# Transposing transfers for two of twelve pairs in a fused linear-attention and MLP kernel

## The chip, the cores and the metric

The kernel runs on one core of a Trainium2 chip. Its engines are TensorE (PE in the profile, its weight loads PEld), VectorE (DVE), ScalarE (ACT), GpSimd (POOL) and SyncE (SP), which here only issues transfers. The metric is device time in microseconds. Every engine works through its own list of instructions in order; they meet through semaphores.

## The reference, cut to what matters

First a recurrent attention with a decaying state, over 4 batches, 8 heads, 768 steps and head size 48, then an MLP with a cosine gate over the 3072 tokens:

```
for t in range(S):
    state = alpha[:, :, t, :, None] * state + einsum('bhd,bhe->bhde', k[:, :, t], v[:, :, t])
    y[:, :, t] = einsum('bhd,bhde->bhe', q[:, :, t], state)

x = y as (3072 tokens, 384)
h = x @ w_in            # 384 -> 2048
g = h * cos(h)
out = g @ w_out         # 2048 -> 384
```

## The kernel before, in words

The work is cut into 12 pairs J = 0 to 11, three to a batch. A pair is 256 steps, two chunks c = 0, 1 of 128; each of the 128 partitions holds two neighbouring steps, its parities e = 0, 1, so partitions 0 to 63 are chunk 0 and 64 to 127 chunk 1. The "ninth pair" is J = 8, the "eleventh" J = 10. For each pair:

- `load` (L105) brings alpha, k, q and v, 384 KB each, on SyncE's queue.
- `ln`, `cums`, `icp` and `exps` (L139 to L208) turn alpha into cumulative products and their inverses. From pair 3 on, the four exponentials of a pair and the logarithm of the next form one session on ScalarE (`eb`), between two loads of function tables.
- `scale_k` (L212) and `scale_q` (L216) multiply k and q by these into bf16 tiles `kh` and `qh`, on POOL or VectorE. There are three buffers of each, 64 columns a head, of which 16 stay zero.
- `trans` (L253 to L261) transposes k and q on TensorE: 4 head pairs x 2 parities x 2 chunks each, 32 transposes into a PSUM tile `T_ps`. `evict_T` (L266) copies each half to the SBUF tile `qkT` (three buffers), on VectorE or ScalarE.
- `scores` (L274) multiplies k by q out of `qkT`, `mask` (L279) evicts them, `outer` (L291) makes the outer products of k and v, `add_state` and `decay_state` (L305 to L313) carry the state.
- `stack_v` (L225) rearranges v by four transfers of 64 KB on SyncE's queue (`vs`).
- `yT` (L340) sums state and score parts, and reads q from `qkT`; `evict_y` (L351) writes the MLP's input.
- `mlp1` (L361), `cosine` (L367), `gate` (L372) and `mlp2` (L390) do the MLP, in four groups of 512 hidden columns. `evict_o` (L402) copies the 384 output columns of each half out of the single PSUM bank "o", into one of four `o_sb` buffers, and `store` (L408) writes 192 KB on SyncE's queue.

PSUM tag "h" is a ring of three two-bank tiles, taken in the order of the calls. `T_ps`, the scores, U, y and the four h tiles of every pair go through it, so a tile waits until the one three places before it has been read.

The order of all work is written out by hand. `PLAN` (L433 on) gives every step of every pair a number; all steps are sorted by it and called in that order, and this is the order of each engine's list, SyncE's among them. The numbers are no times of the chip, only an order. A letter behind a number picks the engine.

Around the two edited places the order of SyncE's list is: load v of pair 11, store of pair 3 half 0, vs of pair 7, store of pair 3 half 1, vs of pairs 8 and 9, store of pair 4 half 1, load k of pair 11, store of pair 5 half 0, vs of pair 10.

Of the kernel before, what the change touches and what calls it, by code (L numbers as in the profile page):

```python
# [10 lines left out]
BF = mybir.dt.bfloat16  # L11
AF = mybir.ActivationFunctionType
ALU = mybir.AluOpType
# [3 lines left out]
def kernel(  # L17
# [10 lines left out]
    nc = tc.nc  # L28
    B, H, S, D = q.shape
    DM, DF = moe_w_in.shape  # L30
    C = 128
    HC = C // 2
# [3 lines left out]
    NP = H // 2  # L36
# [7 lines left out]
    NL, NQ, NV, NS = 4, 3, 3, 2  # L44
    BUF = {"a": 4, "in": 3, "cp": 3, "qkT": 3, "A": 2, "un": 4, "us": 2, "c": 3, "xT": 3, "g": 4}

    consts = ctx.enter_context(tc.tile_pool(name="consts", bufs=1))
    sb = ctx.enter_context(tc.tile_pool(name="sb", bufs=2))
# [15 lines left out]
    for c in range(2):  # L64
        r = slice(HC * c, HC * c + HC)
# [4 lines left out]
    ident_bf = consts.tile([C, C], BF, tag="ident_bf")  # L70
# [8 lines left out]
    lna_t, qh_t, kh_t, vp_t, vs_t = [], [], [], [], []  # L79
    for lst, nm, n in ((lna_t, "lna", NL), (kh_t, "kh", NQ), (qh_t, "qh", NQ), (vp_t, "vp", NV)):  # L80
        for r in range(n):
            t = consts.tile([C, 2, H, 64], BF, tag=f"{nm}{r}", name=f"{nm}{r}")
            nc.vector.memset(t[:, :, :, D:64], 0.0)
            lst.append(t)
    for r in range(NS):
        t = consts.tile([C, 2, H, 64], BF, tag=f"vs{r}", name=f"vs{r}")
        nc.gpsimd.memset(t[:, :, :, D:64], 0.0)
# [9 lines left out]
    a_sb, kqv, cp_sb, icp_sb, qkT_sb, A_sb, c2_sb = {}, {}, {}, {}, {}, {}, {}  # L97
# [73 lines left out]
    def two_banks(name):  # L171
        return ps.tile([C, 2, 512], FP, tag="h", name=name, bufs=3)
# [36 lines left out]

    def scale_k(J, e, eng):  # L210
        icp_ = icp_sb.pop((J, e)).rearrange("p (h d) -> p h d", h=H)
        eng.tensor_tensor(out=kh_t[J % NQ][:, e, :, 0:D], in0=kqv["k", J][:, :, e], in1=icp_, op=ALU.mult)  # L212

    def scale_q(J, e, eng):
        cp = cp_sb[J, e][:, 0:HD].rearrange("p (h d) -> p h d", h=H)
        eng.tensor_tensor(out=qh_t[J % NQ][:, e, :, 0:D], in0=kqv["q", J][:, :, e], in1=cp, op=ALU.mult)  # L216

    def cast_v(J):
        nc.gpsimd.tensor_copy(out=vp_t[J % NV][:, :, :, 0:D].rearrange("s e h d -> s h e d"), in_=kqv.pop(("v", J)))  # L219
# [18 lines left out]
    def evict_vs(J, copy):  # L238
        copy(out=vs_t[J % NS][:, :, :, 0:D],
             in_=vs_ps.pop(J)[:, :, 0:HD].rearrange("s c (h d) -> s c h d", h=H))  # L240
# [12 lines left out]
    def trans(J):  # L253
        T_ps[J] = ps.tile([C, 2, 2 * NP, 2, HC], BF, tag="h", name="T_ps", bufs=3)
        for i, x in ((1, kh_t[J % NQ]), (0, qh_t[J % NQ])):
            for p in range(NP):
                for e in range(2):
                    for c in range(2):
                        r = slice(HC * c, HC * c + HC)
                        nc.tensor.transpose(T_ps[J][:, c, i * NP + p, e, :],  # L260
                                            x[r, e, 2 * p : 2 * p + 2, :].rearrange("s h d -> s (h d)"), ident_bf[r, r])  # L261

    def evict_T(J, c, copy):
        if J not in qkT_sb:
            qkT_sb[J] = sb.tile([C, 2, 2 * NP, C], BF, tag="qkT", name="qkT", bufs=BUF["qkT"])
        copy(out=qkT_sb[J][:, c], in_=T_ps[J][:, c].rearrange("r n e s -> r n (e s)"))  # L266
# [16 lines left out]
    def outer(J):  # L283
        n = 2 if J % NJB < NJB - 1 else 1
        kh, vp = kh_t[J % NQ], vp_t[J % NV]
        U_ps[J] = two_banks("U_ps")
        for p in range(NP):
            for e in range(2):
                for c in range(n):
                    r = slice(HC * c, HC * c + HC)  # L290
                    nc.tensor.matmul(  # L291
                        U_ps[J][:, c, 2 * p * D : 2 * (p + 1) * D].rearrange("r (a d) -> r a d", a=2),
                        kh[r, e, 2 * p : 2 * p + 2, :].rearrange("s h d -> s (h d)"),
                        vp[r, e, 2 * p : 2 * p + 2, 0:D], start=(e == 0), stop=(e == 1))

    U_new = {}
# [50 lines left out]
    def evict_y(J, c, copy):  # L347
        if J not in xT:
            xT[J] = sb.tile([C, KT, T2], BF, tag="xT", name="xT", bufs=BUF["xT"])

        copy(out=xT[J][:, :, c * C : (c + 1) * C].rearrange("r i (t e) -> r i e t", e=2),  # L351
             in_=y_ps[J][:, c, 0 : KT * C].rearrange("r (i e t) -> r i e t", i=KT, e=2))
# [59 lines left out]
    def idle(n):  # L412
# [5 lines left out]
    copies = {"DVE": nc.vector.tensor_copy, "ACT": nc.scalar.copy}  # L418
    mults = {"DVE": nc.vector, "POOL": nc.gpsimd}
    steps = {  # L420
        "load": lambda J, nm: load(nm, J), "w1": load_w1, "w2": load_w2,
        "mula": mul_a, "ln": ln, "cums0": cums0, "cums": cums, "sub": sub, "icp": icp, "exps": exps, "eb": session,
        "sk": lambda J, e, eng="POOL": scale_k(J, e, mults[eng]), "sq": lambda J, e, eng="POOL": scale_q(J, e, mults[eng]),
        "castv": cast_v, "vst": stack_v, "vpe": stack_v_pe,
        "vev": lambda J, eng="DVE": evict_vs(J, copies[eng]), "decay": decay, "trans": trans,
        "evT": lambda J, c, eng="DVE": evict_T(J, c, copies[eng]), "scores": scores, "mask": mask, "outer": outer,
        "add": add_state, "state": decay_state, "yT": yT, "evy": lambda J, c, eng="ACT": evict_y(J, c, copies[eng]),
        "m1": mlp1, "sin": cosine, "gate": gate, "m2": mlp2, "evo": lambda J, c, eng="ACT": evict_o(J, c, copies[eng]),
        "out": store, "idle": idle,
# [68 lines left out]
    }  # L498
    IDLE = [(1501, 16), (7915, 1), (9416, 8), (12569, 4), (14554, 5), (16389, 3), (18254, 3)]

    order = []
    for key, line in PLAN.items():
        kind, *rest = key.split()
        for J, word in enumerate(line.split()):
            if word != "-":
                t, _, eng = word.partition(":")
# [38 lines left out]
```

## Time and profile before

| what | value |
| --- | --- |
| median of 3 runs | 188.16 us (187.92 to 188.28) |
| span of the profiled execution, first to last instruction | 186.5 us |
| median of the runs less that span | 1.66 us |
| TensorE busy | 176.7 us, 95% |
| VectorE busy | 135.4 us, 73% |
| ScalarE busy | 126.5 us, 68% |
| GpSimd busy | 77.1 us, 41% |
| transposes L260 | 384, in groups of 32 |
| evictions L266 | VectorE 16, mean 678 ns; ScalarE 8, mean 1015 ns |
| transfers vs<-vp on SyncE | 36, 64 KB each, 2.1 us to landing |
| stores on SyncE | 23, 192 KB each, 2.6 us to landing |
| granted TensorE clock | 1.000 |

The profiled execution's own time on the device is given by its span only; the median is of other executions of the same program. Groups of instructions are named by line, engine and operation, with what is written before the arrow and what is read behind it. Times in a timeline or a chain count from the start of the span. The chain of waits is found backwards from the last instruction: at each step to what released it, or to the instruction before it on its engine. Transfers issued by SyncE appear as SPq; their duration there is that of the issue and not of the transfer.

### The profile page before, as it was taken

The page shows a single profiled execution, that of the slowest core. Times are in us where ns is not written, and L with a number is a line of the kernel's source. Part 1 is how long each engine was busy: PE and PEld are TensorE (multiplying, and loading weights), DVE is VectorE, ACT ScalarE, POOL GpSimd, SP SyncE. Part 2 cuts the span into 40 slices and gives each one's busy share as a digit, 9 for nine tenths or more (in the row PEclk, how much of TensorE's full clock was granted, in tenths as well). Part 3 has the DMA queues.
Part 4 walks back from the last instruction along what each step waited for, and adds up shares of the span by engine and source line. Part 5 has one row for each costly group of instructions (what it writes and reads, how often), then busy time and mean ns, then how long its engine had stood idle before and what let it go on. Part 6 is the DMA issues. An engine that isn't in the chain of part 4 may idle for free.

```text
span 186.5 us, 5746 instructions
## 1 busy us (share of the span) xinstructions
PE 176.7 (95%) x2467; PEld 126.4 (68%) x2469; DVE 135.4 (73%) x184; ACT 126.5 (68%) x161; POOL 77.1 (41%) x110
## 2 busy tenths in 40 slices
PE   7988799989989999999999999999999999999993
PEld 2434588655667786785688668676867686786872
DVE  7178775589799979698847987794977556754461
ACT  2466876889498986889668999728965264373330
POOL 5079510257645653781896076930360320100000
PEclk9999999999999999999999999999999999999999
DMA  6999999999949979996799932600041005301102
GB/s 152 261 258 165 181 204 237 259 266 265 274 105 304 264 180 245 264 260 167 186 278 278 247 104 46 182 0 4 4 136 47 5 0 158 118 0 66 64 0 84
DMA packets 60137, 29.47 MB, mean 158 GB/s; under 512 B 51024, under 2 KB 60112, under 8 KB 60112
## 3 DMA queue, kind: packets, MB, share of 16 engines
q1 hardware_dynamic: 56256, 25.86, 57.2%
q0 software_dynamic: 3712, 3.15, 11.0%
q8 instruction: 19, 0.31, 0.7%
q10 hardware_dynamic: 144, 0.10, 0.2%
q14 instruction: 6, 0.05, 0.1%
HBM read 25.17 MB, written 4.72 MB: 160 GB/s over the span
## 4 chain that ended last, share of the span: by engine, by line
PE 73%; ACT 15%; DVE 8%; issue 3%; DVEq 0%
PE h_ps L361 31%; PE o_ps L390 24%; PE idle_ps L416 4%; PE y_ps L340 3%; ACT qkT L266 3%; DVE gsb L372 3%; PE T_ps L260 2%; ACT c_sb L367 2%; PE A_ps L274 2%; ACT L136 2%; ACT cp L200 2%; PE U_ps L291 2%; DVE kh L212 2%; ACT icp L192 2%; PE o_last L384 1%
## 5 line engine op out<-in xcount | busy, mean ns | idle before, releaser
L372 DVE TENSOR_TENSOR gsb<-h_ps,c_sb 128x1024 bf16<-128x1024 f32 x48 | 58.1, 1221 | 21.9 <-ACT c_sb L367 21.2
L367 ACT ACTIVATE c_sb<-h_ps,halfpi 128x1024 bf16<-128x1024 f32 x48 | 53.0, 1113 | 26.8 <-PE h_ps L361 23.0
L361 PE MATMUL h_ps<-xT,w 128*128 128x256 bf16 x576 | 66.7, 273 | 1.3 <-ACT xT L351 0.7
L390 PE MATMUL o_ps<-w,gsb 128*128 128x384 bf16 x368 | 66.7, 327 | 0.1
L361 PEld LDWEIGHTS <-w 128*128 128x128 bf16 x576 | 55.6, 98 | 10.1 <-issue 1.6
L390 PEld LDWEIGHTS <-gsb 128*128 128x128 bf16 x368 | 33.8, 98 | 21.2 <-DVE gsb L372 0.6
L313 POOL TENSOR_TENSOR un<-us,c 128x384 bf16<-128x384 f32 x20 | 16.7, 835 | 40.7 <-DVE us L305 29.1
L279 DVE TENSOR_TENSOR A_sb<-A_ps,msk 128x1024 bf16<-128x1024 f32 x24 | 28.9, 1215 | 1.7 <-PE A_ps L274 1.7
L212 POOL TENSOR_TENSOR kh<-k,icp 128x384 bf16<-128x384 f32 x17 | 16.9, 999 | 9.2 <-ACT icp L192 7.8
L216 POOL TENSOR_TENSOR qh<-q,cp 128x384 bf16<-128x384 f32 x15 | 15.0, 1006 | 11.8 <-ACT cp L200 11.8
L149 POOL TENSOR_TENSOR a<-a 128x384 f32<-128x384 f32 x9 | 9.0, 1001 | 12.6 <-DMA a<-in_alpha_dram 12.6
L219 POOL CAST vp<-v 128x768 bf16<-128x768 f32 x12 | 10.1, 841 | 8.8 <-DMA v<-in_v_dram 7.7
L416 PE MATMUL idle_ps<-zeros 128*128 128x512 bf16 x38 | 12.0, 457 | 1.4 <-DVE zeros L52 1.2
L141 ACT ACTIVATE lna<-a 128x768 bf16<-128x768 f32 x12 | 10.2, 847 | 4.6 <-DMA a<-in_alpha_dram 4.6
L266 ACT COPY qkT<-T_ps 128x1024 bf16<-128x1024 bf16 x8 | 8.0, 1015 | 6.9 <-PE T_ps L260 4.4
L136 ACT ACT_TABLE_LOAD x9 | 11.5, 1283 | 0.9 <-PEq L529 0.7
L367 ACT ACT_TABLE_LOAD x9 | 11.5, 1283 | 0.2
L266 DVE COPY qkT<-T_ps 128x1024 bf16<-128x1024 bf16 x16 | 10.8, 678 | 1.1 <-ACT qkT L266 1.1
L305 DVE TENSOR_TENSOR us<-U_ps,un 128x384 f32<-128x384 f32 x16 | 8.7, 550 | 3.8 <-PE U_ps L291 2.8
L402 DVE COPY o_sb<-o_ps 128x384 f32<-128x384 f32 x12 | 6.6, 551 | 6.5 <-PE o_ps L390 6.5
L351 ACT CAST xT<-y_ps 128x384 bf16<-128x384 f32 x12 | 6.7, 594 | 5.6 <-PE y_ps L340 3.8
L351 DVE CAST xT<-y_ps 128x384 bf16<-128x384 f32 x12 | 6.8, 584 | 4.7 <-PE y_ps L340 2.9
(69 smaller groups left out, 159.1 us busy)
## 6 DMA issues: line engine op xcount, KB each, us to landing
k<-in_k_dram SPq DMA_DIRECT2D x12, 384.0 KB, 6.0
a<-in_alpha_dram SPq DMA_DIRECT2D x12, 384.0 KB, 6.1
v<-in_v_dram SPq DMA_DIRECT2D x12, 384.0 KB, 6.0
q<-in_q_dram SPq DMA_DIRECT2D x12, 384.0 KB, 6.3
out_dram<-o_sb SPq DMA_DIRECT2D x23, 192.0 KB, 2.6
vs<-vp SPq DMA_DIRECT2D x36, 64.0 KB, 2.1
w<-in_moe_w_out_dram POOLq DMA_DIRECT2D x4, 384.0 KB, 10.1
w<-in_moe_w_in_dram POOLq DMA_DIRECT2D x4, 384.0 KB, 7.3
```

The source lines that it names most:

```text
L136: nc.scalar.preload_act_table_set("natural_log_exp_and_others")
L212: eng.tensor_tensor(out=kh_t[J % NQ][:, e, :, 0:D], in0=kqv["k", J][:, :, e], in1=icp_, op=ALU.mult)
L216: eng.tensor_tensor(out=qh_t[J % NQ][:, e, :, 0:D], in0=kqv["q", J][:, :, e], in1=cp, op=ALU.mult)
L266: copy(out=qkT_sb[J][:, c], in_=T_ps[J][:, c].rearrange("r n e s -> r n (e s)"))
L279: nc.vector.tensor_tensor(out=A_sb[J][:, c].rearrange("s a p t -> s (a p) t"), in0=A_ps.pop((J, c)).rearrange("s a p t -> s (a p) t"), in1 ...
L313: nc.gpsimd.tensor_tensor(out=u, in0=U_sum.pop(n), in1=c2_sb[J][:, :, c].unsqueeze(3).to_broadcast([C, NP, 2, D]), op=ALU.mult)
L351: copy(out=xT[J][:, :, c * C : (c + 1) * C].rearrange("r i (t e) -> r i e t", e=2), in_=y_ps[J][:, c, 0 : KT * C].rearrange("r (i e t) -> ...
L361: nc.tensor.matmul(h_ps[J, u][:, f, :], w1[:, kk, ft * C : (ft + 1) * C], xT[J][:, kk, :], start=(kk == 0), stop=(kk == KT - 1))
L367: nc.scalar.activation(out=c_sb[J, u], in_=h_ps[J, u], func=AF.Sin, bias=halfpi, scale=1.0)
L372: nc.vector.tensor_tensor(out=gsb[J][:, u * FW : (u + 1) * FW], in0=h_ps.pop((J, u)), in1=c_sb.pop((J, u)), op=ALU.mult)
L390: nc.tensor.matmul(o_ps[J, c][:, 0:DM], gsb[J][:, ft, c * C : (c + 1) * C], w2[:, ft], start=(ft == 0), stop=(ft == NF - 1))
L416: nc.tensor.matmul(idle_ps[0], zeros[:, 0:C], zeros, start=True, stop=True)
```

## The change

For pairs 8 and 10, `trans` and both `evict_T` are struck from the plan. In their place four transfers a pair on SyncE's queue, each of which transposes 64 partitions by 1024 columns of `kh` or `qh` (one chunk, all heads and parities) straight into `qkT`. Their source must lie in blocks of 128 columns, each of one head pair and parity, so `kh` and `qh` get a new layout, pair, parity, head, for all twelve pairs, and every step that touches them is written for it (`scale_q` like `scale_k` below; `trans` and `outer` read `x[r, p, e]`). The ten other pairs keep their transposes on TensorE.

```
-            t = consts.tile([C, 2, H, 64], BF, tag=f"{nm}{r}", name=f"{nm}{r}")
+            t = consts.tile([C, 2, H, 64] if nm in ("lna", "vp") else [C, H, 2, 64], BF, ...)
             nc.vector.memset(t[:, :, :, D:64], 0.0)
-            lst.append(t)
+            lst.append(t.rearrange("s (p e) a d -> s p e a d", p=NP) if nm in ("kh", "qh") else t)
...
-        eng.tensor_tensor(out=kh_t[J % NQ][:, e, :, 0:D], in0=kqv["k", J][:, :, e], in1=icp_, op=ALU.mult)
+        eng.tensor_tensor(out=kh_t[J % NQ][:, :, e, :, 0:D], in0=kqv["k", J][:, :, e].rearrange("p (n a) d -> p n a d", a=2),
+                          in1=icp_.rearrange("p (n a) d -> p n a d", a=2), op=ALU.mult)
...
+    def trans_dma(J, x, c):
+        if J not in qkT_sb:
+            qkT_sb[J] = sb.tile([C, 2, 2 * NP, C], BF, tag="qkT", name="qkT", bufs=BUF["qkT"])
+        r = slice(HC * c, HC * c + HC)
+        i, src_t = {"k": (1, kh_t), "q": (0, qh_t)}[x]
+        nc.sync.dma_start_transpose(
+            out=qkT_sb[J][:, c, i * NP : (i + 1) * NP, :].rearrange("r n (e s) -> r (n e) s", e=2),
+            in_=src_t[J % NQ][r].rearrange("s p e a d -> s (p e a d)"))
...
-        "trans": "14073 17773 40885 47348 58944 70064 80866 92234 109989 116249 127239 136001",
-        "evT 0": "14773:A 18473:A 41585 48048 60976 71899 81566:A 93894 111044 116949:A 129834 138061",
-        "evT 1": "16453:A 19403:A 43330 48048:A 59896 72979 81586 93289 112124 117657 128759 137201:A",
+        "trans": "14073 17773 40885 47348 58944 70064 80866 92234 - 116249 - 136001",
+        "evT 0": "14773:A 18473:A 41585 48048 60976 71899 81566:A 93894 - 116949:A - 138061",
+        "evT 1": "16453:A 19403:A 43330 48048:A 59896 72979 81586 93289 - 117657 - 137201:A",
...
+        "tr k 0": "- - - - - - - - 96950 - 116500 -",
+        "tr q 0": "- - - - - - - - 97000 - 116550 -",
+        "tr k 1": "- - - - - - - - 96951 - 116501 -",
+        "tr q 1": "- - - - - - - - 97001 - 116551 -",
```

More of the change, by code (lines that the diff above doesn't have):

```diff
@@ L81 @@
         for r in range(n):
-            t = consts.tile([C, 2, H, 64], BF, tag=f"{nm}{r}", name=f"{nm}{r}")
+            t = consts.tile([C, 2, H, 64] if nm in ("lna", "vp") else [C, H, 2, 64], BF, tag=f"{nm}{r}", name=f"{nm}{r}")
             nc.vector.memset(t[:, :, :, D:64], 0.0)
-            lst.append(t)
+            lst.append(t.rearrange("s (p e) a d -> s p e a d", p=NP) if nm in ("kh", "qh") else t)
     for r in range(NS):
@@ L211, in scale_k @@
         icp_ = icp_sb.pop((J, e)).rearrange("p (h d) -> p h d", h=H)
-        eng.tensor_tensor(out=kh_t[J % NQ][:, e, :, 0:D], in0=kqv["k", J][:, :, e], in1=icp_, op=ALU.mult)
+        eng.tensor_tensor(out=kh_t[J % NQ][:, :, e, :, 0:D], in0=kqv["k", J][:, :, e].rearrange("p (n a) d -> p n a d", a=2),
+                          in1=icp_.rearrange("p (n a) d -> p n a d", a=2), op=ALU.mult)
     def scale_q(J, e, eng):
         cp = cp_sb[J, e][:, 0:HD].rearrange("p (h d) -> p h d", h=H)
-        eng.tensor_tensor(out=qh_t[J % NQ][:, e, :, 0:D], in0=kqv["q", J][:, :, e], in1=cp, op=ALU.mult)
+        eng.tensor_tensor(out=qh_t[J % NQ][:, :, e, :, 0:D], in0=kqv["q", J][:, :, e].rearrange("p (n a) d -> p n a d", a=2),
+                          in1=cp.rearrange("p (n a) d -> p n a d", a=2), op=ALU.mult)
     def cast_v(J):
@@ L260, in trans @@
                         nc.tensor.transpose(T_ps[J][:, c, i * NP + p, e, :],
-                                            x[r, e, 2 * p : 2 * p + 2, :].rearrange("s h d -> s (h d)"), ident_bf[r, r])
+                                            x[r, p, e].rearrange("s a d -> s (a d)"), ident_bf[r, r])
+    def trans_dma(J, x, c):
[6 more added lines that the diff above has]
+            in_=src_t[J % NQ][r].rearrange("s p e a d -> s (p e a d)"))
     def evict_T(J, c, copy):
@@ L292, in outer @@
                         U_ps[J][:, c, 2 * p * D : 2 * (p + 1) * D].rearrange("r (a d) -> r a d", a=2),
-                        kh[r, e, 2 * p : 2 * p + 2, :].rearrange("s h d -> s (h d)"),
+                        kh[r, p, e].rearrange("s a d -> s (a d)"),
                         vp[r, e, 2 * p : 2 * p + 2, 0:D], start=(e == 0), stop=(e == 1))
@@ L425 @@
         "vev": lambda J, eng="DVE": evict_vs(J, copies[eng]), "decay": decay, "trans": trans,
-        "evT": lambda J, c, eng="DVE": evict_T(J, c, copies[eng]), "scores": scores, "mask": mask, "outer": outer,
+        "evT": lambda J, c, eng="DVE": evict_T(J, c, copies[eng]), "scores": scores, "mask": mask, "outer": outer, "tr": lambda J, x, c: trans_dma(J, x, c),
         "add": add_state, "state": decay_state, "yT": yT, "evy": lambda J, c, eng="ACT": evict_y(J, c, copies[eng]),
```

## The prediction, made before the result

> **What bounds the kernel now.** I read the page first, for the bound, then the chain of waits around the two edited places, then SyncE's queue in order of time, because that is where the new transfers go. Shares of the span by engine and line, and the busy row (busy us, share, instructions):
>
> ```profile
> PE 176.7 (95%) x2467; PEld 126.4 (68%) x2469; DVE 135.4 (73%) x184; ACT 126.5 (68%) x161; POOL 77.1 (41%) x110
> ...
> PE 73%; ACT 15%; DVE 8%; issue 3%; DVEq 0%
> ```
>
> TensorE is the bound on average. But the two pairs lie in different stretches. The chain of waits in order of time (start, us, what):
>
> ```profile
> 104.17 1.11 ACT c_sb L367
> ...
> 111.47 1.28 ACT L136
> ...
> 116.51 1.12 ACT c_sb L367
> 117.63 0.02 issue
> 117.66 2.37 DVE gsb L372 x2
> 120.02 0.04 issue
> 120.06 0.64 PE T_ps L260 x32
> ...
> 130.92 0.33 PE A_ps L274 x8
> 131.25 0.47 PE T_ps L260 x32
> 131.72 0.23 PE A_ps L274 x8
> ```
>
> From 104.17 to 117.63 the chain runs through ScalarE (cosines, the sessions of pairs 9 and 10, four table loads), then through two gates on VectorE, and only at 120.06 back to TensorE, at pair 9's transposes. Pair 8's transposes (113.34 to 113.92 in TensorE's timeline) lie beside that ScalarE stretch; pair 10's, at 131.25, lie on the TensorE chain, which runs unbroken to 183.4. SyncE's queue (start, us, line, what):
>
> ```profile
> 99.49 1.58 SPq L105 DMA_DIRECT2D q<-in_q_dram  x1
> 101.12 1.31 SPq L105 DMA_DIRECT2D v<-in_v_dram  x1
> 102.52 1.23 SPq L408 DMA_DIRECT2D out_dram<-o_sb  x1
> 103.85 2.40 SPq L225 DMA_DIRECT2D vs<-vp  x4
> 106.34 0.53 SPq L408 DMA_DIRECT2D out_dram<-o_sb  x1
> 106.92 8.91 SPq L225 DMA_DIRECT2D vs<-vp  x8
> 115.92 0.53 SPq L408 DMA_DIRECT2D out_dram<-o_sb  x1
> 116.50 0.46 SPq L105 DMA_DIRECT2D k<-in_k_dram  x1
> 117.05 0.76 SPq L408 DMA_DIRECT2D out_dram<-o_sb  x1
> ```
>
> By the order of PLAN, pair 8's four transfers stand right behind the load of v for pair 11 (101.12) and ahead of the store of pair 3, half 0 (102.52). Pair 10's stand behind the store at 117.05; the next entry is vs of pair 10, which starts only at 135.36.
>
> **Removed.** Twice 32 transposes. Pair 8's cost TensorE 0.58 us (they start at 113.34, the h matmuls behind them at 113.92), pair 10's 0.47 us. Four evictions of 0.66 to 0.69 us on VectorE (114.45, 115.51, 132.56, 133.62), and two uses of the three-slot PSUM ring "h".
>
> Pair 8 gains nothing. TensorE stood 0.30 us at 120.06 for the gate on VectorE, which stood for ScalarE; without pair 8's transposes it stands about 0.88 us there instead, because the next tile still takes the slot that the same gate frees. The two evictions end at 116.18, and VectorE then waits 1.48 us for the cosine anyway. This 0.88 us is useful only as cover for a delay.
>
> Pair 10: from 120.06 on nothing but TensorE is on the chain, so its 0.47 us comes off the end. Its evictions lie beside that work: 0.
>
> In the trace 32 transposes take 0.47 to 0.64 us together, pipelined, and that is what I subtract. [...]
>
> **Changed layout.** k and q are scaled into tiles ordered pair, parity, head. The same 8 runs of 48 elements are written per partition, so I take the POOL rows (0.99 to 1.01 us) and VectorE rows as they are: 0. Bounds: -0.1 and +0.2 us, the second if the handful of such operations on the chain (L212 and L216 on VectorE, 2% each at most) grew by a twentieth.
>
> **Added waits on TensorE.** Scores of these pairs now wait for transfers, two for each half. The trace shows a separate wait instruction on TensorE's sequencer at L260 at 51 ns; four for pair 10 at worst cost 0.2 us, at best they hide under running matmuls. I take 0.05.
>
> **Added on SyncE.** Eight transfers of 64 partitions x 1024 bf16 = 128 KB. The trace shows no transposing transfer, so issue time T and transfer time D need bounds. Issue: rows give 0.37 us (a 384 KB load with 1,024 packets, unhindered) to 0.60 us (vs<-vp, the nearest: 64 partitions, bf16, SBUF to SBUF, 64 KB). By bytes, two of the latter are 1.2 us. The transfer has 8 blocks of 128 columns; were each block issued like one vs<-vp, T would be 8 x 0.6 = 4.8 us. So T lies between 0.37 and 4.8; I take about 1.0, between one and two vs<-vp, since issues here do not grow with bytes or packets. Transfer: 512 KB a pair at the 0.26 MB/us that the loads reach is 2.0 us.
>
> Inputs: pair 8's last kh is done on POOL at 101.1 us and SyncE comes free at 102.43: no wait. Pair 10's last qh ends at 121.24, so there the queue waits from 117.8 to 121.24 with nothing due behind it until vs of pair 10 at 135.36. Its results are read by scores at 140.29: 19 us for 4T + D. Pair 8's are read at 122.05: 19.6 us. Both hidden up to T of about 4 us. The qkT ring of three is free in time (pair 8 takes pair 5's, pair 10 takes pair 6's).
>
> What is queued behind matters more. The store of pair 3, half 0 (3/0), frees the o_sb buffer that the copy of pair 5, half 0, on VectorE takes at 108.41; the store now lands at 102.52 + 4.7 = 107.2. That copy frees the single o_ps bank, and TensorE reuses it at 109.74. New landing: issue at 102.43 + 4T plus 2.6 us (the page's landing for stores), or by the rings 106.9 (the v load lands 5.8 after 101.12) + 2.0 + 0.75 for its own 192 KB = 109.7. With T = 1.0 the first is 109.0, so the rings decide: the copy ends at 110.3, TensorE is 0.5 us late, and the 0.88 us of cover at 120.06 swallows that. ScalarE's cosine at 116.51 has 1.8 us to spare over its matmuls. Next in line, vs of pair 7: last issue moves from 105.65 to about 109, lands 2.0 to 2.7 later at 111.7, needed at 112.44. Covered too, barely. Store 3/1 and vs of pairs 8 and 9 are not due before 115.
>
> **Sum**: pair 8 0, pair 10 -0.47, waits +0.05, layout 0, queue 0: -0.4 us. The profiled execution's span is 186.5, so 186.1; the 1.66 us between span and the median of the runs, 188.16, is kept: 187.7 us.
>
> **Rivals.** (a) *The queue is late (slower).* Place: the copy at 108.41 and the o_ps bank. Price: everything beyond 109.74 + 0.88 + 0.42 = 111.0 for the end of that copy is lost one for one; in terms of T, 102.43 + 4T + 2.6 + 0.6 passes this at T = 1.35 us, or D at 3.0 us instead of 2.0. At T = 2 the copy ends at 113.6, 2.6 us past the point: 190.8. For it: the DMA share is 0.9 up to 107 us and issues just ahead took 1.2 to 1.6 us. Against: vs<-vp at 0.6 us each right behind.
>
> (b) *Issue goes by block.* T = 4.8: the store is issued at 121.6, the copy ends at 124.8, 13.8 us past the point: about 202. For it: transposing is the one thing no row shows. Against: no issue row above 2.7 us, backed up.
>
> [...]
>
> (c) *Issue slower still*, say twice by block, T = 9.6: 4 x 9.6 - 5.4 = 33 us past the point, 221, and more once pair 10's transfers pass 19 us. Only the size against every row speaks against it.
>
> (d) *No change.* Pair 10's 0.47 us is given back to waits (all four at 51 ns) or to ScalarE and VectorE behind it: 188.1. For it: VectorE and ScalarE wait on one another through the whole second half. Against: h and o matmuls have 1.4 us of idle in the whole span.
>
> **How the numbers follow.** A measurement of this kernel tells apart about 0.2%, 0.38 us. Forecast, transfers hidden and pair 10's time gained: 0.38, at 187.7 (its own range 187.3 to 187.9). Above-plan gain, when pair 8's 0.58 counts too, 187.1: 0.02. No change: 0.10. Queue late, 188.6 to 192: 0.30, nearly as much as the forecast, because the copy at 108.41 has hardly any room. By block, to 202: 0.13. Beyond: 0.07. So faster 0.40, same 0.10, slower 0.50, though no single slower case is likelier than the forecast. The range takes in all but the by-block cases and the tail: 187.1 to 192.0.
>
> **What would show it.** Right: SyncE's row of transposing transfers near 1 us each; the store behind them landing by 110; no idle above 0.5 us before o_ps at L390 near 110; ScalarE's chain unmoved at 116.5 and TensorE waiting about 0.9 us for a gate near 120; scores of pair 10 without a wait, 0.4 us earlier. Wrong: the copy of pair 5 on VectorE waiting for the store's transfer, y of pair 7 waiting for vs, or scores waiting for qkT. The forecast fails first if T exceeds 1.35 us.

## The result, and the profile after

The changed kernel takes 189.67 us (median of 5 runs) against 188.28 us of the kernel before beside it: ratio 1.0069, 95% interval 1.0047 to 1.0090. One of the five, 192.93 us, showed a lower granted clock (0.991) and stays out of the ratio. In a later session the change gave 1.0046 (1.0028 to 1.0064). It is slower by about half a percent, 0.9 to 1.3 us, where 0.4 us of gain was forecast. The profiled execution has a span of 188.5 us against 186.5.

The page of the changed kernel, its busy row:

```profile
PE 175.1 (93%) x2403; PEld 125.2 (66%) x2405; DVE 132.6 (70%) x180; ACT 126.6 (67%) x161; POOL 77.4 (41%) x110
```

TensorE does 1.6 us less and ends 2.0 us later. What it waited for between 95 and 188 us (total, times, longest):

```profile
PE y_ps L351 <- DMA vs<-vp: 1.2, 2, 0.9
...
PE h_ps L372 <- issue: 0.8, 1, 0.8
...
PE o_ps L401 <- ACT o_sb L413: 0.6, 1, 0.6
...
PE o_ps L401 <- DVE gsb L383: 0.4, 1, 0.4
```

Before, TensorE waited for none of these; only the "issue" one was there, with 0.12 us, and a wait of 0.30 us for a gate at 120.06. (Lines after 270 moved by 11: L401 after is L390 before.) The second half of the MLP on TensorE serves as milestones, before (the first line is that wait):

```profile
120.06 0.41 PE L260 MATMUL T_ps<-ident_bf,kh 64*128 64x64 bf16 x16 [0.30 <-DVE gsb L372]
...
122.98 1.48 PE L390 MATMUL o_ps<-w,gsb 128*128 128x384 bf16 x8
...
131.87 1.48 PE L390 MATMUL o_ps<-w,gsb 128*128 128x384 bf16 x8
...
141.93 2.11 PE L390 MATMUL o_ps<-w,gsb 128*128 128x384 bf16 x12
144.70 0.82 PE L390 MATMUL o_ps<-w,gsb 128*128 128x384 bf16 x4
```

and after:

```profile
104.58 0.81 PE L401 MATMUL o_ps<-w,gsb 128*128 128x384 bf16 x4
...
114.44 0.29 PE L351 MATMUL y_ps<-A_sb,vs 128*32 128x128 bf16 x5 [0.87 <-DMA vs<-vp]
115.11 0.57 PE L351 MATMUL y_ps<-A_sb,vs 128*32 128x128 bf16 x27 [0.38 <-DMA vs<-vp]
...
124.22 1.47 PE L401 MATMUL o_ps<-w,gsb 128*128 128x384 bf16 x8
...
132.64 1.47 PE L401 MATMUL o_ps<-w,gsb 128*128 128x384 bf16 x8
...
143.46 2.11 PE L401 MATMUL o_ps<-w,gsb 128*128 128x384 bf16 x12 [0.61 <-ACT o_sb L413]
...
146.66 0.82 PE L401 MATMUL o_ps<-w,gsb 128*128 128x384 bf16 x4 [0.36 <-DVE gsb L383]
```

Read as differences, after less before:

| milestone | lag | step | what lies between |
| --- | --- | --- | --- |
| o at 104.58 (103.97 before) | 0.61 | 0.61 | 0.80 us "issue" in front of h matmuls at 100.0, 0.12 before; ahead of every edited step |
| o at 124.22 | 1.24 | 0.63 | y of pair 7 waits 1.25 us for vs, and its matmuls take 0.4 us longer around these waits; 0.58 us of transposes and the 0.30 us wait at 120.06 are gone |
| o at 132.64 | 0.77 | -0.47 | pair 10's transposes are gone |
| o at 143.46 | 1.53 | 0.76 | o waits for the copy of the o_ps bank on ScalarE |
| o at 146.66 | 1.96 | 0.43 | the gate behind that copy is late too |

The last two rows are the surprise: 1.2 us are lost near 143 us, some 16 us after the last added transfer has been issued (127.03). SyncE's queue after:

```profile
103.33 3.48 SPq L270 DMA_TRANSPOSE qkT<-kh  x2
106.85 2.59 SPq L270 DMA_TRANSPOSE qkT<-qh  x2
109.48 0.58 SPq L419 DMA_DIRECT2D out_dram<-o_sb  x1
110.17 3.38 SPq L227 DMA_DIRECT2D vs<-vp  x4
...
121.16 2.60 SPq L270 DMA_TRANSPOSE qkT<-kh  x2
123.85 3.18 SPq L270 DMA_TRANSPOSE qkT<-qh  x2
136.51 2.39 SPq L227 DMA_DIRECT2D vs<-vp  x4
138.99 2.87 SPq L419 DMA_DIRECT2D out_dram<-o_sb  x3
```

Pair 8's four transfers hold the queue for 6.15 us. At 138.99 three stores take 2.87 us to issue, 1.53 us before. The first of them is pair 5, half 1; its buffer is the one that ScalarE's copy of pair 7, half 1, writes next. The view of `o_sb` in a window around them (issue durations in ns, min, median, max; time to landing min, median, max), after, and then the landing of the same three before:

```profile
L419 SPq DMA_DIRECT2D out_dram<-o_sb x3: 397/542/1732, 139.0 to 140.1; - x3
...
DMA to landing us min/median/max: 3.7/3.7/3.9
```

```profile
DMA to landing us min/median/max: 2.0/2.0/2.1
```

ScalarE's copy, after and then before:

```profile
142.93 0.48 ACT L413 COPY o_sb<-o_ps 128x384 f32<-128x384 f32 x1 [3.09 <-PE h_ps L372]
```

```profile
140.03 0.48 ACT L402 COPY o_sb<-o_ps 128x384 f32<-128x384 f32 x1 [0.95 <-DMA out_dram<-o_sb]
```

The profile puts the 3.09 us down to TensorE, but the copy starts just behind the store's landing (138.99 + 3.87 = 142.86 us), and in the repeated change the same wait, 3.3 us, is put down to the store. In the tenth of a microsecond from 140.0 the transfer view of the changed kernel shows what is new (queue, packets, MB, share):

```profile
q8 instruction: 1, 0.02, 92.2%
```

That is one packet of 16,384 bytes on the queue that the profile names "instruction" (an instruction packet from here on), starting at 140.02 and running 1.48 us. In the kernel before the packet of the same number, the fifteenth, starts at 132.39, where no other transfer runs (132 to 134 us hold this packet alone). In the changed kernel the rate is then low for a microsecond, 12 GB/s on average from 141.15 to 142.35 us, near the 11 GB/s that the packet itself reaches, 16,384 bytes in 1.48 us (mean GB/s in 40 slices of 138 to 144 us, after):

```profile
GB/s 14 41 177 184 34 0 177 212 48 0 109 191 130 219 358 328 328 379 348 348 256 10 0 10 10 10 10 20 20 317 369 348 287 41 20 10 0 0 0 0
```

So I formed a theory, E below: these packets fetch TensorE's code, its list is 128 instructions shorter, and so they come at other moments; one of them now meets the store, the DMA engine that carries it brings its share of the store late, the copy waits, and the only o_ps bank with it. (What the packets carry is read from the queue's name; that one engine is late is the theory's reading of the rate, and no view here shows the engines one by one.)

### The profile page after: what moved, and what is told of

Read it like the earlier page. It is cut to its first block, busy times and chain, and to the rows that moved or that the text cites. A ratio compares the mean times of both kernels' runs of the same rounds, so it can differ in the third digit from the quotient of the medians.

```text
span 188.5 us, 5632 instructions
## 1 busy us (share of the span) xinstructions
PE 175.1 (93%) x2403; PEld 125.2 (66%) x2405; DVE 132.6 (70%) x180; ACT 126.6 (67%) x161; POOL 77.4 (41%) x110
## 4 chain that ended last, share of the span: by engine, by line
PE 60%; ACT 12%; issue 9%; DVE 8%; DMA 6%; SPq 3%; POOL 1%; POOLq 0%; DVEq 0%; ACTq 0%
PE h_ps L372 29%; PE o_ps L401 19%; ACT qkT L277 4%; DMA a<-in_alpha_dram 3%; PE y_ps L351 3%; SPq L227 2%; DMA out_dram<-o_sb 2%; DVE gsb L383 2%; PE U_ps L302 2%; PE T_ps L262 2%; ACT c_sb L378 2%; PE A_ps L285 2%; PE o_last L395 1%; ACT lna L141 1%; ACT cp L200 1%
## 5 line engine op out<-in xcount | busy, mean ns | idle before, releaser
L401 PE MATMUL o_ps<-w,gsb 128*128 128x384 bf16 x368 | 66.7, 326 | 1.0 <-ACT o_sb L413 0.6
L401 PEld LDWEIGHTS <-gsb 128*128 128x128 bf16 x368 | 33.8, 98 | 22.4 <-DVE gsb L383 1.1
L427 PE MATMUL idle_ps<-zeros 128*128 128x512 bf16 x38 | 10.9, 424 | 1.4 <-DVE zeros L52 1.2
L413 ACT COPY o_sb<-o_ps 128x384 f32<-128x384 f32 x11 | 5.3, 477 | 8.4 <-PE o_ps L401 5.2
L277 DVE COPY qkT<-T_ps 128x1024 bf16<-128x1024 bf16 x12 | 8.1, 679 | 3.0 <-ACT qkT L277 3.0
```

The costliest lines, as they stand in the source:

```text
L401: nc.tensor.matmul(o_ps[J, c][:, 0:DM], gsb[J][:, ft, c * C : (c + 1) * C], w2[:, ft], start=(ft == 0), stop=(ft == NF - 1))
L413: copy(out=t, in_=o_ps.pop((J, c))[:, 0:DM])
```

## The experiments

Theories at the start: A, pair 8's place in SyncE's queue is the cost and pair 10 gains 0.47 us; B, the new layout costs; C, transposing transfers disturb whatever runs beside them; D, pair 8's transposes count as gain too. E as above, F: pair 10's time is taken back by ScalarE or VectorE; G: the store is late from the transfers or its place. Ratios are against the kernel before on the same chip, with their 95% intervals.

| run | ratio | interval |
| --- | --- | --- |
| layout alone | 0.9997 | 0.9983 to 1.0011 |
| pair 8 alone | 1.0017 | 1.0000 to 1.0034 |
| pair 10 alone | 0.9993 | 0.9976 to 1.0009 |
| no transposes for 8 and 10 | 1.0021 | 1.0006 to 1.0035 |
| the same, store moved | 0.9976 | 0.9962 to 0.9990 |
| kernel before, store moved | 0.9993 | 0.9976 to 1.0010 |
| the change, store moved | 0.9983 | 0.9969 to 0.9998 |
| the change, pair 8 behind vs | 1.0025 | 1.0006 to 1.0044 |
| both | 0.9972 | 0.9959 to 0.9986 |
| the change again | 1.0046 | 1.0028 to 1.0064 |
| the change, list padded | 0.9987 | 0.9969 to 1.0004 |
| three pairs, store moved | 0.9935 | 0.9914 to 0.9955 |

**The parts one by one.** Each is the changed kernel with some pairs put back:

```
-        "tr k 0": "- - - - - - - - 96950 - 116500 -",      # and the three other rows
+        "tr k 0": "- - - - - - - - - - - -",               # layout alone; trans and evT as before
+        "tr k 0": "- - - - - - - - 96950 - - -",           # pair 8 alone
+        "tr k 0": "- - - - - - - - - - 116500 -",          # pair 10 alone
```

> Only the new layout of kh and qh; all twelve pairs are transposed on TensorE as before. A (the place in SyncE's queue): 188.2 us, no change, since no transfer is added. B (the layout itself costs): 189.3 to 189.7, the whole of the change. C (transposing transfers disturb whatever runs beside them, wherever they stand): 188.2.

> Pair 8 alone by transposing transfers, pair 10 on TensorE. A: vs of pair 7 lands 6.2 us later and y of pair 7 waits for it about 1.2 us; without the 0.47 us that pair 10 would gain this is slower than the change itself, 189.8 to 190.2. B: 189.3 to 189.7. C: half of the loss, about 188.9.

> Pair 10 alone by transposing transfers, pair 8 on TensorE. A: nothing due stands behind these transfers, so TensorE's 0.47 us comes off the end: 187.7 to 187.9, no wait for qkT before scores of pair 10. B: 189.3 to 189.7. C: about 188.9.

> Leaves out the transposes of pairs 8 and 10 altogether: their scores and y read qkT of the pair before (7 and 9), so neither TensorE, VectorE nor a transfer makes them. This is the change with costless transfers. A: 187.6 to 187.8, pair 10's 0.47 us only; pair 8's 0.58 us turns into a longer wait of TensorE near 120 us. Rival D (pair 8's time counts too): 187.1. B: 189.

The fourth run replaces the transfers by an alias of the neighbour's tile:

```
+        "alias": lambda J: qkT_sb.__setitem__(J, qkT_sb[J - 1]),
```

B falls: the layout costs nothing that shows, at most 0.11% by its interval. Pair 8 alone costs 0.17%, with an interval that reaches down to nothing, and not the 0.8 to 1% that A expected; pair 10 alone gains 0.07%, which its interval does not tell from nothing or from 0.2%. C expected 1.003 of each and is not borne out for pair 10. The sum of the two, 1.001, is far from the change's 1.0046 to 1.0069, so something happens only when both are taken off TensorE. The fourth run, in which scores and y of the two pairs read the tile of the pair before, shows that part of it needs no transfer at all: with costless transposes the kernel is slower than before. A and D cannot explain that. In its window of 134 to 145 us the same late stores stand:

```profile
L419 SPq DMA_DIRECT2D out_dram<-o_sb x3: 407/530/1585, 137.5 to 138.6; - x3
L413 ACT COPY o_sb<-o_ps x1: 479/479/479, 141.2 to 141.2; 128x384 f32<-128x384 f32 x1
...
DMA to landing us min/median/max: 3.5/3.5/3.7
```

There the instruction packet starts at 138.69. With only one pair taken off TensorE it starts at 136.1 (pair 8 alone) or 135.7 (pair 10 alone), some 3.5 us further on from 132.4 for each pair taken off, and the three stores land in 2.0 us.

**The store moved.** One number: the store of pair 5, half 1, goes from behind vs of pair 10 to behind the store of its half 0 (and, where they are there, pair 10's transfers), where it lands long before it is needed.

```
-        "out 1": "44770 66136 87674 100827 112274 133721 136121 ...
+        "out 1": "44770 66136 87674 100827 112274 117000 136121 ...
```

> As the run without the transposes of pairs 8 and 10 (their scores read the pair before), and the store of pair 5, half 1, is issued behind the store of its half 0 instead of behind vs of pair 10. E (a 16 KB fetch of TensorE's code, moved by the missing instructions, holds up one DMA engine while this store is under way, and ScalarE's copy waits for it): the wait near 141 us goes and pair 10's 0.47 us stays: 187.8 to 188.0 against 188.3 before. F (pair 10's time is taken back elsewhere, by ScalarE or VectorE): 188.5 to 188.9, as without the move.

> The kernel before with this one store moved, nothing else. E: 188.3, no change: its 0.9 us wait on ScalarE near 140 us lies beside TensorE's work. F: 188.3 too. If the store alone were worth something, 187.8.

> The change with pair 8's four transfers put behind vs of pairs 7 and 8 in SyncE's queue, and the store moved. E: no wait of y of pair 7 and none near 141 us: 187.8 to 188.0. F: 188.5 to 188.9.

> The change as it is, with the store moved alone. E: the wait near 141 us goes (0.6 us on TensorE and 0.4 behind it), y of pair 7 still waits for vs: 188.6 to 189.0 against 189.6 of the change. F: 189.6.

Moving this store is worth 0.45% without transposes (1.0021 to 0.9976) and nothing to the kernel before (0.9993). The change itself goes from 1.0046 or 1.0069 to 0.9983, better than the 188.6 to 189.0 that I expected, which was reckoned from the change's profile alone. So F falls: once the copy does not wait for this store, pair 10's time stays. Without transposes the gain is 0.24% (0.10 to 0.38), or 0.45 us, against 0.47 us read off the chain. The two stores left in the old place still land late, in 3.1 to 4.2 us in the three runs with the store moved and both pairs off TensorE against 2.0 to 2.1 in the kernel before with the store moved, and TensorE waits for neither: what matters is that the one needed store is late.

**Pair 8 behind vs.** In the "both" row above and alone here:

```
-        "tr k 0": "- - - - - - - - 96950 - 116500 -",
+        "tr k 0": "- - - - - - - - 102100 - 116500 -",     # behind vs of pair 8; the three others alike
```

> Pair 8's transfers behind vs of pairs 7 and 8; the store stays behind vs of pair 10. E: y of pair 7 does not wait, but the fetch still meets the store: 188.6 to 189.2, between the change and the run with the store moved. If pair 8's place in the queue were the main cost: 187.8 to 188.0.

With the store left in its place this is 1.0025, the same as costless transposes (1.0021): ScalarE's copy waits 2.9 us for the store and TensorE 0.4 and 0.4 us. With the store moved it is 0.9972 against 0.9983 with pair 8 in front; the medians differ by 0.29 us, the intervals overlap, and so what pair 8's place costs then is not resolved. In "both", TensorE's list shows the cover that the prediction had reckoned at 0.88 us near 120 us, as 0.19 and 0.63:

```profile
118.82 0.50 PE L302 MATMUL U_ps<-vp,kh 64*128 64x96 bf16 x8 [0.19 <-DVE gsb L383]
119.95 0.41 PE L262 MATMUL T_ps<-ident_bf,kh 64*128 64x64 bf16 x16 [0.63 <-DVE gsb L383]
```

**The packets moved, nothing else.** Theory E was put to the test without touching a transfer: small matmuls on zeros at the start bring TensorE's list back to its old length (68 matmuls and their weight loads come in, 4 long ones and theirs go: 128 more).

```
-    IDLE = [(1501, 16), ...
+    IDLE = [(1501, 12), ...        # and 68 of the following behind them
+            nc.tensor.matmul(idle_ps[0][0:64, 0:32], zeros[:, 0:64], zeros[:, 0:32], start=True, stop=True)
```

> The changed kernel again, beside the three others of this call. E and its rivals: 189.4 to 189.8, with the fetch of TensorE's code near 140 us and the late store.

> The change with 68 small matmuls on zeros (64 columns by 32) in place of 4 of the 16 long idle ones of the first 7 us, so that TensorE's list is again as long as before, 4,940 instructions, and its code is fetched at the same instructions as before from pair 10 on. Stores and transfers stay where the change has them. E: the fetch moves to about 132 us, the store lands in 2.0 us, no wait near 141: 188.1 to 188.7. G (the store is late for another reason, by the transposing transfers or by its place in the queue): 189.4 to 189.8.

The change as it is: 1.0046. Padded: 0.9987, with the same transfers and stores in the same places. The instruction packet starts at 132.34 again, and the window of 137 to 144 us reads

```profile
L419 SPq DMA_DIRECT2D out_dram<-o_sb x3: 385/395/533, 138.2 to 139.3; - x3
L413 ACT COPY o_sb<-o_ps x1: 478/478/478, 140.4 to 140.4; 128x384 f32<-128x384 f32 x1
...
DMA to landing us min/median/max: 2.0/2.0/2.1
```

G falls. The pads moved another packet as well: at 110.55 in the repeated change it ran while vs of pair 7 was issued, which took 3.61 us, and TensorE waited 1.4 us for vs; padded, the packets stand at 106.65 and 114.97, vs takes 2.40 us and TensorE waits 0.2 us. In the first profile of the change this packet is at 111.40, and one vs transfer takes 1.55 us to issue instead of 0.59. The kernel before has a packet at 110.47 too, but its vs of pair 7 is issued before, from 103.85 to 106.25: here the packet stayed, and pair 8's transfers pushed vs into it. Part of what looked like pair 8's price thus went with a packet too, and padding takes it away with the rest; the change with the store moved, where vs of pair 7 still meets a packet (110.34), is the run that shows the late store alone. The first sums start at 8.77 us with the pads and at 7.12 us in the kernel before; the kernel before with the same pads, below (0.9990), shows that this does not reach the end.

**The reverse, in a kernel without transposing transfers.** The kernel before, with 68, 80 and 88 pads in place of the same 4 long matmuls and no other edit.

> The kernel before, with the same 68 small matmuls in place of 4 long idle ones at the start: 128 instructions more on TensorE and no transposing transfer anywhere. By the shift seen so far (64 instructions move a fetch by about 3.3 us) the fetch of 145.1 us falls at about 138.5, on the stores. E: the store lands 1.5 to 2 us later, ScalarE waits about 3 us for it, and the kernel is slower by what the change lost there: 188.8 to 189.3. If the late store needs the transposing transfers: 188.3.

> The kernel before with 80 small matmuls in place of 4 long idle ones. With 68 the fetch fell at 140.2 us, just behind the first of the three stores; 24 instructions more should bring it to about 139.2. E: the store of pair 5, half 1, lands in 3.5 to 4 us, ScalarE waits about 3 us, 188.8 to 189.2 against 188.4 before. If a late store alone costs nothing without the transfers: 188.4.

> The same with 88 small matmuls, 40 instructions more than with 68: fetch at about 138.5, as the first store is issued. E: as with 80, 188.8 to 189.2, unless the fetch is over before the store's packets run. Otherwise 188.4.

With 68 the packet came at 140.16, behind the needed store: that landed in 2.1 us, the two after it in 3.5, and the time did not move (0.9990, 0.9974 to 1.0006). With 80 it came at 138.58; the needed store landed in 3.0 us, ScalarE waited 1.8 us, TensorE not at all, 1.0010 (0.9992 to 1.0027). With 88 it came at 137.36, on vs of pair 10, whose issue took 2.92 us; 1.0027 (1.0008 to 1.0045), with no wait on TensorE that explains it. So without any transposing transfer, too, small transfers were late where an instruction packet met them (3.0 and 3.5 us to landing against 2.0, 2.92 us of issue against 2.39), as E says, but these three kernels did not reproduce the whole loss: the needed store took at most 0.9 us longer to land, where the change's took 1.8 and, repeated, 2.0 us longer. With 80 the copy ended at 142.12 and TensorE came to the bank at 142.70, so there was still room; in the change TensorE would have come there near 142.85, and the copy ended at 143.41. That the packet alone can cost the kernel before 0.4% stays unshown, and the 0.27% with 88 stays open.

**The price of the queue and of a transfer.**

```
+    for x in "kq":                                     # pair 8's transfers, a second time
+        for c in (0, 1):
+            PLAN[f"tr {x} {c}  "] = "- - - - - - - - 96960 - - -"
```

> Pair 8 alone by transposing transfers, each issued twice (the second writes the same values), all ahead of vs of pair 7. A (every us of queue beyond the cover is lost): four more at 1.3 us each put vs 5.2 to 5.4 us later and the time at 193.5 to 194.5, from 188.7 with four. If the queue's place costs little even then: under 190.

1.0495 (1.0451 to 1.0540), 197.84 us: 3 to 4 us more than expected, and 9.1 us more than with four transfers. The eight hold the queue from 103.30 to 116.85, 13.55 us where four held it for some 6 us, and TensorE waits 7.0 us for vs. About 2 us of the queue are of this experiment's own making: the second transfers of a tile were not issued until the first had landed (SyncE waits 1.4 us for `qkT<-kh` and 0.6 us for `qkT<-qh`), which the expectation lacked. It also lacked what the table by stretch shows (length, busy time of PE, PEld, DVE, ACT, POOL with instructions, granted clock, DMA share, GB/s):

```profile
110.00:114.00 4.00, 3.73 (x53) 2.20 (x51) 3.28 (x4) 3.96 (x5) 1.72 (x2) 1.00 0.71 82
114.00:118.00 4.00, 0.00 (x0) 0.00 (x0) 0.00 (x0) 3.24 (x6) 3.87 (x5) 0.82 0.59 92
...
121.00:123.00 2.00, 1.60 (x35) 1.14 (x31) 0.47 (x1) 0.00 (x0) 0.98 (x2) 0.50 0.56 164
...
125.00:127.00 2.00, 2.00 (x12) 1.46 (x11) 0.66 (x1) 1.11 (x1) 0.00 (x0) 0.55 0.57 146
```

With TensorE idle for 7 us, its granted clock is 0.82 in 114 to 118, 0.50 from 118 to 125, 0.55 in 125 to 127 and 1.00 after that; the 36 h matmuls from 122.48 on take 6.16 us, 4.04 in the changed kernel. Beyond its cover, then, the queue did cost, and here, with 7.5 us more of queue for 9.1 us more of time, more than 1:1.

> Pair 10 alone, by eight transfers of 64 KB instead of four of 128 KB. If the issue goes by size: 0.6 to 0.7 us each. If it is a price of the transfer: 1.25 us each, as for 128 KB. The time itself 187.9 to 188.4 either way.

```
+        for z in range(2):
+            w = slice(2 * z, 2 * z + 2)                # two head pairs a transfer, pair 10 alone
```

The time was 188.77 us, from a single run. The issues (ns, min, median, max), with 64 KB each:

```profile
L272 SPq DMA_TRANSPOSE qkT<-kh x4: 1228/1243/1288, 119.1 to 123.0; - x4
L272 SPq DMA_TRANSPOSE qkT<-qh x4: 1188/1247/2014, 124.4 to 128.2; - x4
```

The 128 KB ones of the change have a median of 1.27 us. Between these two sizes the issue was a price of the transfer, not of its bytes; for pair 10's 512 KB, eight transfers held the queue for 11.1 us (119.12 to 130.21) and four for 5.9 (121.16 to 127.03).

**A version that beats both.** Pair 9 joins, with its transfers at 116400, ahead of pair 10's; pair 8's stand behind vs; the store is moved.

> Pairs 8, 9 and 10 by transposing transfers, pair 8's behind vs of pair 8, pair 9's ahead of pair 10's, the store moved. Pair 9's transposes stand on the chain at 120.06 behind a wait of 0.30 us, so E expects a further 0.6 to 0.9 us: 187.0 to 187.4, if their transfers (issued from 119 us) land before its scores at 130.85; 2 us slower if they do not.

187.14 us, ratio 0.9935 (0.9914 to 0.9955): 1.2 us faster than the kernel before. Pair 9's transposes stood on the chain at 120.06 behind a wait for the gate; both are gone. All twelve transfers are issued between 109.4 and 131.0 us, TensorE stands nowhere for qkT, and its one wait between 95 us and the end is 0.2 us for a gate.

## Why the prediction was wrong

*Right.* The bound and its two stretches: pair 10's 0.47 us came off between 124 and 132 us to the hundredth, and pair 8's 0.58 us became a longer wait for the gate (0.82 us in "both" against 0.30). The layout cost nothing. Neither pair's scores waited for qkT. That pair 8's place in the queue is a risk was right too, at another spot than rival (a) named: vs of pair 7, called "Covered too, barely", was not covered in the change, and TensorE waited 1.25 us for it, one of the named signs of being wrong. That used up the cover at 120 us: there TensorE did not wait at all.

*Mis-sized: T.* Taken as 1.0 us and measured 1.25 to 2.17; the four of pair 8 took 6.15 us, past the 5.4 (4 x 1.35) named as the failing point. The median of 1.27 is not between one and two vs<-vp but a little above two, 1.2, so "about 1.0" was short by a quarter even with room in the queue.

*Failed: the copy at 108.41.* I had the store 3/0 free the buffer of that copy, by counting four buffers around. The copy ran at 109.02, ahead of that store's issue at 109.48, and did not wait:

```profile
109.02 0.55 DVE L413 COPY o_sb<-o_ps 128x384 f32<-128x384 f32 x1
```

A pool that hands out the buffer freed first would explain it; that buffer would be store 4/0's, issued at 95.51. No run tests this. The price of rival (a), the range's upper end and the point 1.35 us were reckoned from a dependency that is not there, so it is in good part luck that 189.67 us lies inside the range.

*Failed: the term "queue 0".* This is the step that turned the sign. The prediction looked for late transfers only right behind the added ones, up to about 115 us, and put the rest of SyncE's queue at nothing. Of the 1.8 us that the profile of the change lost between 105 and 147 us, pair 10's gain aside, 0.6 us is at vs of pair 7, behind pair 8's transfers; 1.2 us stands behind none of the added transfers. Taking 128 instructions off TensorE moved the instruction packets, the fifteenth from 132.39 to 140.02, and it met the store that ScalarE, and through the o_ps bank TensorE, needed at 140 us. Moving that store ahead of vs of pair 10, or moving the packets by padding, each turns 1.0046 into 0.998 to 0.999. Before the change ScalarE's copy already waited 0.9 us for this store: a wait off the chain, whose copy ended at 140.51, 1.4 us before TensorE's next o matmuls at 141.93, and I read past it. Rival (d), time given back behind pair 10, had the right place, but not the way.

*Not of the change.* The 0.61 us ahead of 104 us in the profiled execution is a wait without a visible releaser at 100.0; with the layout alone it is 0.41, with pair 10 alone 0.42, and 0.42 in the kernel before with only the store moved, where all up to there is the same as before. In the repeated change it was 0.3. Without it the profile's 2.0 us are 1.35, near the 0.9 to 1.3 us of the runs.

## What to carry to other kernels

Before moving work off the bound engine, list the waits on the other engines that are met with under a microsecond to spare, and the small transfers behind them: in this kernel a tuned order stayed tuned only as long as nothing shifted under it. When two harmless parts together cost something that neither costs alone, run the change with the work simply left out; if that is slower too, the cost is not in what was added. Issue transposing transfers where the queue has nothing due behind it, at the 1.25 us each that they took here, and first move forward the stores that something waits for.

## What the runs showed of the hardware

- On the queue that the profile names "instruction" (q8) the kernel before and the changed kernel have 19 packets each, of 16,384 bytes and 0.88 to 1.66 us. The one at 132.39 us in the kernel before came at 135.7 and 136.1 with 64 instructions fewer on TensorE (pair 10 or pair 8 alone), at 138.69 and 140.02 with 128 fewer (no transposes, the change), and at 132.34 in the change padded by 128. That the packets are TensorE's is inferred from this.
- Where such a packet met them, 192 KB stores landed in 3.0 to 3.9 us (3.0 with 80 pads, 3.5 with 68, 3.5 to 3.7 without transposes, 3.7 to 3.9 in the change) against 2.0 to 2.1 for the same stores in the kernel before, and vs of a pair, four transfers of 64 KB, took 2.9 to 3.6 us to issue against 2.4 (2.92 with 88 pads, 3.00 with pair 8 alone, 3.38 in the change, 3.61 in its repeat).
- A transposing transfer of 64 partitions by 512 or 1024 bf16 took 1.24 to 1.28 us to issue (medians), up to 2.17 us right behind a load of v, and landed 2.3 to 5.6 us after its issue.
- In the run with pair 8's transfers twice, TensorE had no matmuls for 7.0 us (113.7 to 120.8); its granted clock was 0.82 on average in 114 to 118, 0.50 from 118 to 125, 0.55 in 125 to 127, and 1.00 after that.
